# Splitting the second-layer matmuls of the two later parts into two 64-row matmuls with a PSUM bank each

## The chip, the cores and the metric

The kernel runs on one core of one Trainium2 chip. The metric is the device time of one execution in microseconds (us); lower is better.

## What is computed

The reference has two steps. The first is attention over q, k and v of shape (4, 8, 576, 64): four heads look at a local window of 32 positions, four at every 32nd position. The second is a mixture of four experts on the 2304 x 512 result, weighted by normalised domain probabilities. Almost all of the time is in the second step:

```python
p = domain_probs / (domain_probs.sum(-1, keepdims=True) + 1e-09)
for e in range(E):                     # E = 4, D = 512, F = 1024
    h = np.maximum(x @ w1[e], 0.0)     # (2304, 512) @ (512, 1024)
    out += p[:, e:e + 1] * (h @ w2[e]) # (2304, 1024) @ (1024, 512)
```

## The kernel before, in words

**Units and parts.** Each expert's hidden layer is cut into two halves of 512, so there are eight units of weights (a 512 x 512 piece of w1 and one of w2). The 2304 tokens are cut into three parts: a first of 512 tokens and two later ones of 896. The first part goes through all eight units while attention still runs. Then each later part goes through its eight units, so that there are sixteen stages of the kind below.

**Precision.** Every matmul operand is split into a high and a low part in the 4-byte type float32r, and a product is the sum of high x high, high x low and low x high. ScalarE writes the high parts (lines 616, 676, 787), VectorE or GpSimd the low ones (lines 617, 679, 788).

**A stage of a later part** (`plan_unit`, line 818) has two phases on TensorE. In the first phase the first layer is done by a seven-product scheme on quarter blocks (line 811): 7 products x 2 column blocks x 6 matmuls = 84 matmuls of 448 columns. ScalarE and VectorE then finish `h`: 16 tiles of 128 x 448 (four blocks of the hidden axis, two token halves, high and low). In the second phase each of the seven 128-token tiles `t` gets 12 matmuls of 512 columns (`mm2_t`, line 684): four blocks `f` of the hidden axis, three products each, all accumulated in one PSUM bank. The `h` slice is the stationary operand (128 rows x 128 columns), the `w2` block the moving one (128 rows x 512 columns). VectorE then reads the bank, scales it by the token's probability and adds it to `acc` (`accumulate`, line 690). After the last unit of a part SyncE sends `acc` out (line 720). The very last token tile of the kernel is done in two column halves of 256.

**Banks.** PSUM's eight banks are three pools: "mo" with four, "sc" with two and "ps" with two. `next_bank` (line 701) goes round them as mo, ps, mo, sc, and a bank is taken again when what read it is done.

**Order.** The order on every engine is written out ahead. `Plan` (line 32) simulates the engines with a duration and a due time for every operation. TensorE's matmuls of the two layers keep the order in which they are added. On the other engines the operation that can start first goes first, and the due time decides between several. Operations marked "VP" can go to VectorE or to GpSimd, whichever the simulation finishes earlier. The order that comes out is each engine's program.

**Attention** matters here as the only place before the change where matmuls use part of the array. Scores (line 460) are 64-row by 64-column matmuls that alternate between rows and output partitions 0 to 63 and 64 to 127. The value product of the strided heads (line 545) has 54 rows, which start at partition 0 for the first bank and at 64 for the second, and alternates between output partitions 0 to 63 and 64 to 127. The transposes of line 515 use all 128 rows. These operands are plain float32.

Of the kernel before, what the change touches and what calls it, by code (L numbers as in the profile page):

```python
# [31 lines left out]
class Plan:  # L32
# [19 lines left out]
    def add(self, eng, dur, fn, reads=(), writes=(), prio=0.0, bank=None, moe=False, cols=0, xfer=None, two=False, lead=None):  # L52

        o = Op()
        o.eng, o.dur, o.fn, o.prio, o.bank, o.moe = eng, dur, fn, prio, bank, moe  # L60
        o.start = None
        o.cols = cols
        o.xfer = xfer
        o.two = two or eng == "VP"
        o.ready = 0.0
        o.nxt = []
        o.idx = len(self.ops)
        pre = set()
        for r in reads:
            if r in self.writer:  # L70
                pre.add(self.writer[r])
        for w in writes:
            if w in self.writer:
                pre.add(self.writer[w])
            pre.update(self.readers.get(w, ()))
        pre.discard(o)
        for r in reads:
            self.readers.setdefault(r, []).append(o)
        for w in writes:
            self.writer[w] = o  # L80
            self.readers[w] = []
        o.kind, o.lead, o.early = eng, lead, 0.0
        o.wait = o.pre = len(pre)
        for p in pre:
            p.nxt.append(o)
        self.ops.append(o)
# [215 lines left out]
def attn_moe_kernel(  # L302
# [13 lines left out]
    nc = tc.nc  # L316
    B, H, S, D = 4, 8, 576, 64
    NT, DM = out.shape
    E, _, F = w1.shape
# [49 lines left out]
    def bank(key):  # L369
        t = pools[key[0]].tile([P, 512], F32, tag=key[0], name=key[0])  # L370
        held[key] = t
        return t
# [317 lines left out]
    def accumulate(a, g, e, key, first, cs):  # L690
        sc = pr[:, g, e:e + 1]
        a = a[:, cs]
        pt = held[key][:, 0:cs.stop - cs.start]
        if first:
            nc.vector.tensor_scalar_mul(out=a, in0=pt, scalar1=sc)
        else:
            nc.vector.scalar_tensor_tensor(out=a, in0=pt, scalar=sc, in1=a, op0=ALU.mult, op1=ALU.add)  # L697
# [3 lines left out]
    def next_bank():  # L701
        cnt[0] += 1
        return (("sc", "mo", "ps", "mo")[cnt[0] % 4], "s", cnt[0])

    def plan_mm2(key, hh, hl, htok, ts, a, g, e, first, last, z, cs=ALL):
        passes = list(enumerate((i, f) for f in range(NKF) for i in range(3)))
        for o in (0, 6):
            js = passes[o:o + 6]
            need = set()
            for _, (i, f) in js:  # L710
                need.update(htok("hhl"[i], f))
                need.add(f"w2{f}" + "hlh"[i])
            w = (cs.stop - cs.start) / DM
            add("PE", PT * w, lambda js=js: mm2_t(hh(), hl(), ts, js, key, cs), sorted(need), [key], z,
                key if o == 0 else None, True, 3072 * w)
        tok = f"acc{a}{cs.start}"
        toks = [tok] if cs != ALL or a < TB // P - 1 else [f"acc{a}{i}" for i in (0, DM // 2)]
        add("DVE", 0.75, lambda: accumulate(acc[a], g, units[e][0], key, first, cs), [key, "pr"], toks, z + 2 * PT)
        if last:
            add("SP", 0.4, lambda: nc.sync.dma_start(out=out[g * P:g * P + P, cs], in_=acc[a][:, cs]), toks,  # L720
                [f"out{g}{cs.start}"], z + 3, xfer=((0.8 * w, 128),))

    def plan_first(u, z):

        def mm1_op(f, js):
            key = ("mo", "a", u, f)
            need = set()
            for _, (i, c) in js:
                need.add((("a11", "a12"), ("s3", "a22"))[f // 2][c // 2] + "hhl"[i])
                need.update(f"x{'hlh'[i]}{c}{g}" for g in range(2))  # L730
            add("PE", (TA + 32) / 2400 * len(js), lambda: mm1_plain(f, js, key), sorted(need), [key], z,
                key if js[0][0] == 0 else None, True, TA * len(js))

        passes = list(enumerate(PASS if u else PASS0))
        if u == 0:
            for o in range(0, 12, 3):
                for f in range(NKF):
                    mm1_op(f, passes[o:o + 3])
        else:
            for f in range(NKF):  # L740
                mm1_op(f, passes)
        for f in range(NKF):
            key = ("mo", "a", u, f)
            src = lambda key=key: held[key][:, 0:TA]
            add("ACT", 0.62, lambda f=f, src=src: relu_hi(lambda: hs[0][f], src), [key], [f"hh{f}"], z)
            add("DVE", 0.68, lambda f=f, src=src: relu_lo(lambda: hs[1][f], lambda: hs[0][f], src),
                [key, f"hh{f}"], [f"hl{f}"], z)
        for t in range(TA // P):
            plan_mm2(("mo", "b", u, t), lambda: hs[0], lambda: hs[1], lambda j, f: [f"h{j}{f}"],
                     slice(t * P, t * P + P), t, t, u, u == 0, u == NU - 1, z + 11)  # L750
# [67 lines left out]
    def plan_unit(part, u, first, last, z):  # L818
        ka, kb, kc = ([next_bank() for _ in range(2)] for _ in range(3))
        SEQ = (("a11", "b11", ka, 1), ("s1", "t1", kc, 1), ("s2", "t2", ka, 0), ("a12", "b21", kb, 1),  # L820
               ("s3", "t3", ka, 0), ("a22", "t4", ka, 0), ("s4", "b22", kc, 0))
        us = {}

        def copy_u(nm, f, key, zz):
            i = us[nm, f] = ucnt[0] % 4
            ucnt[0] += 1
            add("ACT", 0.55, lambda: nc.scalar.activation(out=late["u"][i], in_=held[key][:, 0:TH], func=AF.Copy),  # L827
                [key, "late2"], [f"u{i}"], zz)

        def finish(f, half, key, nm, zz):  # L830

            cs = slice(half * TH, half * TH + TH)
            hi, lo = (lambda: late["h"][0][f][:, cs]), (lambda: late["h"][1][f][:, cs])
            need = [key]
            src = lambda: held[key][:, 0:TH]
            if nm:
                i = us[nm]
                c = ucnt[1] % 2
                ucnt[1] += 1
                add("DVE", 0.6, lambda: nc.vector.tensor_tensor(  # L840
                    out=late["c"][c], in0=held[key][:, 0:TH], in1=late["u"][i], op=ALU.add), [key, f"u{i}"], [f"c{c}"], zz)
                src = lambda: late["c"][c]
                need = [f"c{c}"]
            add("ACT", 0.52, lambda: relu_hi(hi, src), need + ["late2"], [f"Hh{f}{half}"], zz + 0.6)
            add("DVE", 0.6, lambda: relu_lo(lo, hi, src), need + [f"Hh{f}{half}"], [f"Hl{f}{half}"], zz + 1.1, two=bool(nm))

        for n, (a, b, keys, first_in) in enumerate(SEQ):
            for f in range(2):
                key = keys[f]
                zz = z + (2 * n + f) * PM  # L850
                need = [a + "h", a + "l"] + [f"{b}{h}{j}" for h in "hl" for j in range(2)]
                add("PE", PM, lambda a=a, b=b, f=f, key=key, first_in=first_in: product(a, b, f, key, first_in),
                    need, [key], zz, key if first_in else None, True, 6 * TH)
                ze = zz + PM
                if n == 0:
                    copy_u("p1", f, key, ze)
                elif n == 2:
                    copy_u("u2", f, key, ze)
                elif n == 3:
                    finish(f, 0, key, ("p1", f), ze)  # L860
                elif n == 4:
                    copy_u("u3", f, key, ze)
                    finish(2 + f, 1, kc[f], ("u3", f), ze)
                elif n == 5:
                    finish(2 + f, 0, key, None, ze)
                elif n == 6:
                    finish(f, 1, key, ("u2", f), ze)
        g0 = (TA + (part - 1) * TB) // P
        for t in range(TB // P):
            halves = sorted({t * P // TH, (t * P + P - 1) // TH})  # L870
            end = part == 2 and last and t == TB // P - 1
            for cs in (slice(0, DM // 2), slice(DM // 2, DM)) if end else (ALL,):
                plan_mm2(next_bank(), lambda: late["h"][0], lambda: late["h"][1], lambda j, f, halves=halves: [f"H{j}{f}{x}" for x in halves],
                         slice(t * P, t * P + P), t, g0 + t, u, first, last, z + 14 * PM + 2 * PT * t, cs)


# [142 lines left out]
```

## Time and profile before

| | before |
|---|---|
| median of 3 runs | 837.15 us (836.17 to 837.17) |
| the profiled execution, its own time | 836.88 us |
| its span, first to last instruction | 835.1 us |
| TensorE matmul busy | 826.3 us, 99% of the span, 4953 matmuls |
| VectorE busy | 507.1 us, 61%, 772 instructions |
| ScalarE, GpSimd busy | 325.5 us (39%), 219.4 us (26%) |
| TensorE clock granted | 0.999 of full speed |

How to read it: PE is TensorE's matmuls and PEld its weight loads, which overlap them; DVE is VectorE, ACT ScalarE, POOL GpSimd, SP SyncE. L688 means line 688 of the kernel. Successive matmuls overlap in the records, since each is drawn with its pipeline's tail, so the cadence is read from starts, or from a merged stretch by its count, and not from one matmul's duration. "128*128" behind a matmul is rows by columns of the stationary operand, the shape after it the moving one. A row of the timeline merges neighbours of one kind: start, length of the merged stretch, count at the end.

### The profile page before, as it was taken

What the parts mean: (1) busy time and instruction counts of PE and PEld (TensorE: products, weight loads), DVE (VectorE), ACT (ScalarE), POOL (GpSimd) and SP (SyncE); (2) the same over time, 40 slices, a digit from 0 to 9 for tenths busy, and PEclk for the clock granted to TensorE, in tenths of its full rate; (3) what the DMA queues carried; (4) which work ended last, traced back from release to release, by engine and by line L of the source; (5) the groups of instructions that cost most, each with busy time, mean ns of one, the idle gap of its engine ahead of it and who ended that gap; (6) DMA issues with size and microseconds to landing.
All of it is one profiled execution on the core that took longest, in us unless ns stands there. A gap on an engine that the chain in (4) does not pass through costs nothing.

```text
span 835.1 us, 12327 instructions
## 1 busy us (share of the span) xinstructions
PE 826.3 (99%) x4953; PEld 707.2 (85%) x4953; DVE 507.1 (61%) x772; ACT 325.5 (39%) x606; POOL 219.4 (26%) x187
## 2 busy tenths in 40 slices
PE   8999999999999999999999999999999999999998
PEld 5788887888889888888988889898888988888896
DVE  5987974845546474655747466664646656475552
ACT  4554455533325143351624326152442615234240
POOL 5632232701402130321313042521312213031100
PEclk9999999999999999999999999999999999999999
DMA  9754731323220121111212111111111113111002
GB/s 303 264 187 154 225 110 52 102 101 101 101 76 27 50 100 51 50 51 51 75 46 83 51 51 51 75 64 46 57 50 51 51 51 101 51 51 51 0 1 89
DMA packets 33114, 68.97 MB, mean 83 GB/s; under 512 B 2080, under 2 KB 2464, under 8 KB 33056
## 3 DMA queue, kind: packets, MB, share of 16 engines
q1 hardware_dynamic: 32624, 67.92, 24.1%
q8 instruction: 39, 0.64, 0.3%
q10 hardware_dynamic: 432, 0.26, 0.1%
q14 instruction: 19, 0.16, 0.1%
HBM read 63.45 MB, written 4.72 MB: 82 GB/s over the span
## 4 chain that ended last, share of the span: by engine, by line
PE 96%; DMA 3%; ACT 0%; issue 0%; DVE 0%
PE mo L688 29%; PE mo L811 16%; PE mo L672 10%; PE ps L688 9%; PE sc L688 9%; PE sc L811 8%; PE ps L811 8%; PE sc L460 2%; PE ps L545 2%; PE ps L515 2%; DMA raw<-in_w 1%; DMA vstL<-in_v_local 1%; DMA m_loc<-c_local 0%; ACT xr L592 0%; ACT w2h L616 0%
## 5 line engine op out<-in xcount | busy, mean ns | idle before, releaser
L688 PE MATMUL mo<-w2h,h 128*128 128x512 f32 (+1 forms) x456 | 148.7, 387 | 0.0
L616 ACT ACTIVATE w2h<-raw 128x512 fp32r<-128x512 f32 x88 | 54.9, 631 | 240.5 <-PE mo L688 136.0
L697 DVE SCALAR_TENSOR_TENSOR acc<-mo,pr,acc 128x512 f32<-128x512 f32 (+1 forms) x77 | 57.5, 746 | 89.8 <-PE mo L688 88.8
L688 PEld LDWEIGHTS mo<-w2h,h 128*128 128x128 f32 x456 | 85.4, 188 | 17.4
L679 DVE SCALAR_TENSOR_TENSOR h<-c,h 128x448 fp32r<-128x448 f32 x96 | 93.0, 993 | 6.8 <-ACT h L676 3.4
L688 PE MATMUL mo<-w2l,h 128*128 128x512 f32 (+1 forms) x228 | 88.3, 387 | 0.0
L617 POOL TENSOR_TENSOR w2l<-raw,w2h 128x512 fp32r<-128x512 f32 x25 | 34.0, 1365 | 196.7 <-ACT w2h L616 196.6
L688 PE MATMUL mo<-w2h,hs 128*128 128x512 f32 x256 | 83.0, 395 | 0.0
L617 POOL TENSOR_TENSOR a12l<-raw,a12h 128x512 fp32r<-128x512 f32 x18 | 29.7, 1648 | 167.4 <-ACT a12h L616 135.8
L688 PE MATMUL ps<-w2h,h 128*128 128x512 f32 x224 | 73.5, 389 | 0.0
L688 PE MATMUL sc<-w2h,h 128*128 128x512 f32 (+1 forms) x224 | 72.5, 385 | 0.0
L676 ACT ACTIVATE h<-c 128x448 fp32r<-128x448 f32 x96 | 52.8, 575 | 17.7 <-DVE c L840 15.7
L688 PEld LDWEIGHTS mo<-w2h,hs 128*128 128x128 f32 x256 | 48.0, 188 | 10.3
L617 DVE TENSOR_TENSOR w2l<-raw,w2h 128x512 fp32r<-128x512 f32 x63 | 44.7, 737 | 9.7 <-ACT w2h L616 9.7
L688 PEld LDWEIGHTS mo<-w2l,h 128*128 128x128 f32 x228 | 42.8, 188 | 8.5
L688 PE MATMUL mo<-w2l,hs 128*128 128x512 f32 x128 | 49.9, 390 | 0.0
L688 PEld LDWEIGHTS ps<-w2h,h 128*128 128x128 f32 x224 | 42.1, 188 | 8.7
L688 PEld LDWEIGHTS sc<-w2h,h 128*128 128x128 f32 x224 | 41.9, 188 | 8.4
L827 ACT ACTIVATE u<-mo 128x448 f32<-128x448 f32 x48 | 26.2, 545 | 50.7 <-PE mo L811 50.3
L688 PE MATMUL ps<-w2l,h 128*128 128x512 f32 x112 | 43.6, 389 | 0.0
L688 PE MATMUL sc<-w2l,h 128*128 128x512 f32 (+1 forms) x112 | 43.2, 385 | 0.0
L840 DVE TENSOR_TENSOR c<-mo,u 128x448 f32<-128x448 f32 x48 | 29.5, 615 | 17.7 <-PE mo L811 16.4
(278 smaller groups left out, 1713.0 us busy)
## 6 DMA issues: line engine op xcount, KB each, us to landing
raw<-in_w SPq DMA_DIRECT2D x44, 1024.0 KB, 5.3
qkS<-in_qk_strided SPq DMA_DIRECT2D x16, 329.0 KB, 8.0
out<-acc SPq DMA_DIRECT2D x17, 256.0 KB, 2.0
vstL<-in_v_local SPq DMA_DIRECT2D x8, 432.0 KB, 8.0
vstS<-in_v_strided SPq DMA_DIRECT2D x8, 384.0 KB, 9.0
qkL<-in_qk_local SPq DMA_DIRECT2D x8, 336.0 KB, 7.1
qkL<-in_qk_local SPq DMA_DIRECT2D x8, 272.0 KB, 7.3
out<-acc SPq DMA_DIRECT2D x2, 128.0 KB, 1.7
```

What stands on the lines that cost most here:

```text
L460: nc.tensor.matmul(s[a, o:o + W], lhsT, rhs, start=True, stop=True)
L515: nc.tensor.transpose(pt[0:rows, P * (g - g0):P * (g - g0) + P], src, ident)
L616: add("ACT", 0.62, lambda: nc.scalar.activation(out=hi(), in_=src(), func=AF.Copy), need, [name + "h"], z)
L617: add("VP", VP, lambda e: engine(e).tensor_tensor(out=lo(), in0=src(), in1=hi().bitcast(F32), op=ALU.subtract), need + [name + "h"], [name ...
L672: nc.tensor.matmul(pt[:, 0:TA], w[:, c % 2, (f % 2) * P:(f % 2) * P + P], (xl if i == 1 else xh)[c], start=j == 0, stop=j == 11)
L676: nc.scalar.activation(out=dst(), in_=src(), func=AF.Relu)
L679: nc.vector.scalar_tensor_tensor(out=dst(), in0=src(), scalar=0.0, in1=hi().bitcast(F32), op0=ALU.max, op1=ALU.subtract)
L688: nc.tensor.matmul(pt, ht[f][:, ts], wt[f][:, cs], start=j == 0, stop=j == 11)
L697: nc.vector.scalar_tensor_tensor(out=a, in0=pt, scalar=sc, in1=a, op0=ALU.mult, op1=ALU.add)
L811: nc.tensor.matmul(pt, wq[a][i == 2][:, j, f * P:f * P + P], xq[b][i == 1][j], start=bool(first) and n == 0, stop=True, skip_group_check=True)
L827: add("ACT", 0.55, lambda: nc.scalar.activation(out=late["u"][i], in_=held[key][:, 0:TH], func=AF.Copy), [key, "late2"], [f"u{i}"], zz)
L840: add("DVE", 0.6, lambda: nc.vector.tensor_tensor(out=late["c"][c], in0=held[key][:, 0:TH], in1=late["u"][i], op=ALU.add), [key, f"u{i}"], ...
```

## The change

A later part's token tile now takes two banks. Each of its 12 matmuls is written as two, over rows 0 to 63 and rows 64 to 127 of the same operands. The first accumulates in one bank, the second in the other, and they alternate. VectorE adds both banks to `acc`, one after the other. The first part keeps `plan_mm2`, and the planner is given the same TensorE duration for a pair as for the one matmul before.

```diff
+    def mm2_rows(hh, hl, ts, js, keys, cs):
+        pts = [(held[k] if k in held else bank(k))[:, 0:cs.stop - cs.start] for k in keys]
+        for j, (i, f) in js:
+            ht, wt = ((hh, w2h), (hh, w2l), (hl, w2h))[i]
+            for r, pt in enumerate(pts):
+                rows = slice(64 * r, 64 * r + 64)
+                nc.tensor.matmul(pt, ht[f][rows, ts], wt[f][rows, cs], start=j == 0, stop=j == 11)
+
+    def plan_mm2_rows(keys, hh, hl, htok, ts, a, g, e, first, last, z, cs=ALL):
...
+            if o == 0:
+                add("PE", 0.0, lambda: bank(keys[0]), (), [keys[0]], z, keys[0], True)
+            add("PE", PT * w, lambda js=js: mm2_rows(hh(), hl(), ts, js, keys, cs), sorted(need), list(keys), z,
+                keys[1] if o == 0 else None, True, 3072 * w)
...
+        for i, key in enumerate(keys):
+            add("DVE", 0.75, lambda i=i, key=key: accumulate(acc[a], g, units[e][0], key, first and i == 0, cs), [key, "pr"], toks, z + 2 * PT)
...
-                plan_mm2(next_bank(), lambda: late["h"][0], lambda: late["h"][1], lambda j, f, halves=halves: [f"H{j}{f}{x}" for x in halves],
+                plan_mm2_rows((next_bank(), next_bank()), lambda: late["h"][0], lambda: late["h"][1], lambda j, f, halves=halves: [f"H{j}{f}{x}" for x in halves],
                          slice(t * P, t * P + P), t, g0 + t, u, first, last, z + 14 * PM + 2 * PT * t, cs)
```

## Rows read from the trace of the kernel before

**Rows 1.** The page: span, busy time, and the granted clock in 40 slices.

```profile
span 835.1 us, 12327 instructions
PE 826.3 (99%) x4953; PEld 707.2 (85%) x4953; DVE 507.1 (61%) x772; ACT 325.5 (39%) x606; POOL 219.4 (26%) x187
PEclk9999999999999999999999999999999999999999
```

**Rows 2.** Busy time by phase: a second layer, a first layer, the last first layer.

```profile
core 0: us, PE busy (x) PEld busy (x) DVE busy (x) ACT busy (x) POOL busy (x), PEclk, DMA share, GB/s
269.59:288.64 19.05, 19.05 (x85) 15.77 (x84) 9.55 (x13) 3.26 (x6) 3.18 (x4) 1.00 0.17 56
288.64:305.76 17.12, 17.12 (x86) 15.77 (x85) 12.07 (x18) 10.57 (x21) 4.96 (x4) 1.00 0.19 63
...
794.98:812.09 17.11, 17.11 (x86) 15.76 (x84) 8.46 (x14) 7.58 (x15) 0.89 (x1) 1.00 0.00 1
```

**Rows 3.** Line 688 alone, from the first stage to the last matmul.

```profile
252.48:831.50 579.02, 307.79 (x1357) 253.08 (x1356) 1.00 0.16 54
```

**Rows 4.** The chain that ended last, its final pieces: start us, us, what.

```profile
825.86 2.72 PE mo L688 x12
828.58 1.43 PE sc L688 x12
830.02 1.45 PE mo L688 x12
831.47 0.02 issue
831.49 0.48 DVE acc L697
```

**Rows 5.** The timeline inside a second layer: matmuls and the weight loads beside them.

```profile
599.87 0.19 PEld L688 LDWEIGHTS mo<-w2l,h 128*128 128x128 f32 x1
600.09 0.39 PE L688 MATMUL mo<-w2l,h 128*128 128x512 f32 x1
600.09 0.19 PEld L688 LDWEIGHTS mo<-w2h,h 128*128 128x128 f32 x1
...
600.32 0.39 PE L688 MATMUL mo<-w2h,h 128*128 128x512 f32 x1
```

**Rows 6.** The timeline in attention: partial-array matmuls, and full-row transposes.

```profile
56.67 0.27 PE L515 MATMUL ps<-ident,pmS 128*128 128x128 f32 x1
56.87 1.61 PE L460 MATMUL sc<-qkS 64*64 64x54 f32 x48
...
58.79 0.60 PE L515 MATMUL ps<-ident,pmL 128*96 128x128 f32 x4
...
75.80 0.22 PE L545 MATMUL ps<-pTS,vstS 54*64 54x54 f32 x1
...
35.83 0.80 PE L545 MATMUL ps<-pTS,vstS 54*64 54x54 f32 x28
```

**Rows 7.** The timeline where TensorE goes from line 688 to 545 and back.

```profile
137.54 0.39 PE L688 MATMUL mo<-w2l,hs 128*128 128x512 f32 x1
...
137.76 0.40 PE L688 MATMUL mo<-w2h,hs 128*128 128x512 f32 x1
138.09 0.38 PE L545 MATMUL ps<-pTS,vstS 54*64 54x54 f32 x6
...
139.12 0.40 PE L545 MATMUL ps<-pTS,vstS 54*64 54x54 f32 x8
...
139.45 0.50 PE L688 MATMUL mo<-w2h,hs 128*128 128x512 f32 x1
...
139.78 0.39 PE L688 MATMUL mo<-w2l,hs 128*128 128x512 f32 x1
```

**Rows 8.** Line 697 in the later parts: durations in ns (min/median/max), first and last start.

```profile
L697 DVE SCALAR_TENSOR_TENSOR acc<-mo,pr,acc x51: 483/751/752, 250.0 to 831.5; 128x512 f32<-128x512 f32 x50, 128x256 f32<-128x256 f32 x1
```

More of the change, by code (lines that the diff above doesn't have):

```diff
@@ L721, in plan_mm2 @@
                 [f"out{g}{cs.start}"], z + 3, xfer=((0.8 * w, 128),))
+    def mm2_rows(hh, hl, ts, js, keys, cs):
[6 more added lines that the diff above has]
+    def plan_mm2_rows(keys, hh, hl, htok, ts, a, g, e, first, last, z, cs=ALL):
+        passes = list(enumerate((i, f) for f in range(NKF) for i in range(3)))
+        w = (cs.stop - cs.start) / DM
+        for o in (0, 6):
+            js = passes[o:o + 6]
+            need = set()
+            for _, (i, f) in js:
+                need.update(htok("hhl"[i], f))
+                need.add(f"w2{f}" + "hlh"[i])
+            if o == 0:
+                add("PE", 0.0, lambda: bank(keys[0]), (), [keys[0]], z, keys[0], True)
+            add("PE", PT * w, lambda js=js: mm2_rows(hh(), hl(), ts, js, keys, cs), sorted(need), list(keys), z,
+                keys[1] if o == 0 else None, True, 3072 * w)
+        tok = f"acc{a}{cs.start}"
+        toks = [tok] if cs != ALL or a < TB // P - 1 else [f"acc{a}{i}" for i in (0, DM // 2)]
+        for i, key in enumerate(keys):
+            add("DVE", 0.75, lambda i=i, key=key: accumulate(acc[a], g, units[e][0], key, first and i == 0, cs), [key, "pr"], toks, z + 2 * PT)
+        if last:
+            add("SP", 0.4, lambda: nc.sync.dma_start(out=out[g * P:g * P + P, cs], in_=acc[a][:, cs]), toks,
+                [f"out{g}{cs.start}"], z + 3, xfer=((0.8 * w, 128),))
     def plan_first(u, z):
```

## The prediction, made before the change was run

> **What bounds the kernel now.** I read the page first. TensorE's matmuls are busy 826.3 of 835.1 us at the full clock, and no other engine passes 61% [rows 1]. So the time is the sum of TensorE's cadences, and the question is what a matmul costs in the stretch that changes. The busy times by phase show the pattern there: a second layer lasts 19.05 us and a first layer 17.1 us, TensorE is busy throughout both, and VectorE works 9.55 us of the second layer and 12.07 us of the first [rows 2]. There are sixteen such stages. Line 688 alone accounts for 307.79 us in them, with 1356 matmuls (one more hangs over the window's edge) [rows 3]. Of these 1332 have 512 columns and 24, those of the last token tile, have 256.
>
> The chain that ended last gives the cadence without the overlap in which matmuls are drawn. Twelve matmuls of 512 columns take 2.72 us, 0.2267 us each, and twelve of 256 columns 1.43 to 1.45 us, 0.120 us each [rows 4]. The difference, 0.1067 us for 256 columns, is 0.417 ns per column, so 512 columns take 213.3 ns, and **13.3 ns of each matmul do not depend on its columns**. That is the only part of the cadence that a new way of writing the matmul could save: 1356 x 13.3 ns = 18.0 us. The weight load is not exposed beyond that. Each load of 0.19 us starts together with the matmul before its own (both at 600.09) and ends inside the 0.227 us [rows 5].
>
> **The change, part by part.**
>
> *The pairs.* Each of the 1356 matmuls becomes two with the same columns and half the rows. No row shows this form in float32r. The nearest ones are attention's. There a full-row transpose of 128 columns follows the one before after (0.60 - 0.27) / 3 = 0.11 us, or 0.86 ns per column; by that a 54-column matmul alone would take 46 ns. The 64-row, 64-column matmuls follow each other after (1.61 - 0.22) / 47 = 29.6 ns, so two are in the array at once. In the stretch at 35.83 they follow after (0.80 - 0.22) / 27 = 21.5 ns [rows 6]. One row half holds only two column tiles, so a cadence under half of 46 ns there needs rows from 0 and rows from 64 at work together, into the same output partitions of two banks. That is just what the change writes. I therefore take a pair to last as long as the one matmul did: the two halves stream side by side, each with its 13.3 ns. The term is 0. Its lower bound is -18.0 us, the whole fixed part gone. Its upper bound is one after the other: 1332 x 0.2267 + 24 x 0.120 = +304.8 us. I stay at 0 because it is what the nearest rows show, and the two ends are cases of their own below.
>
> The Trainium skill ("TensorE: Matmul & The Clock Gate", Part 3, "Measured speedup vs the span model") adds about 4 ns for each further tile of a set. By that the sum would be 1356 x 4 ns = 5.4 us higher, an estimate of 848.8 us. No run here shows it for float32r, and the sum goes without it.
>
> *Changing form.* Where TensorE goes from full-row to partial matmuls and back it loses time. The first 54-row matmul starts 0.33 us after the last full one (137.76 to 138.09) instead of 0.227, a loss of 0.10. On the way back the last partial one starts at 139.12 + 0.40 - 0.22 = 139.30 and the full one at 139.45, 0.15 us instead of a pair's 0.06, a loss of 0.09; and the second full one comes 0.33 us after the first instead of 0.227, a loss of 0.10, its load having had nothing to hide behind [rows 7]. I take that last loss for the first pair too. Going in costs 0.20 us and coming out 0.19. Both phases run in order within a stage, so there are 16 ways in and 15 out: 16 x 0.20 + 15 x 0.19 = **+6.05 us**, all on TensorE's path. The bounds are 0 (halves of the rows at full width need no such pause) and twice that, 12.1 us.
>
> *VectorE.* Each token tile gets a second accumulation of 0.75 us [rows 8]: 7 x 0.75 = 5.3 us per second layer, which brings VectorE from 9.55 to 14.8 of 19.05 us. Its idle time hides this, and I cost it at 0. Both accumulations wait for the same last matmul, so the second adds no wait, only 0.75 us to whatever stands behind it: low parts of the next weights, which can go to GpSimd (3.18 us busy there), and the last additions for `h`, needed by the fourth tile, three tiles of 2.72 us after the phase begins. A tile's two banks are asked for again four tiles later, 10.9 us, while the accumulations take 1.5 us. In the last first layer, where VectorE has little help, it works 8.46 of 17.11 us [rows 2]. If one accumulation per stage were uncovered after all, that would be 16 x 0.75 = 12 us; nothing in this part can gain.
>
> *SyncE and the end.* An output waits for both accumulations. Between the parts that puts the weight load behind it in SyncE's queue at most 0.75 us later, which has most of a first layer to spare. At the very end nothing covers it: after the last matmul VectorE does one accumulation of 256 columns, 0.48 us [rows 4], and now two: **+0.48 us**.
>
> *Sum.* 836.88 (the profiled execution; the median of the runs is 837.15, 0.03% above) + 0 + 6.05 + 0 + 0.48 = **843.4 us**. About 0.2% (1.7 us) is what a measurement of this kernel can tell from no change, and this is 0.8%.
>
> **The rivals.**
>
> *Float32r halves do not run together.* A float32r stream takes a column every 0.417 ns, twice the rate of attention's float32 ones at 0.86 ns [rows 4, 6]. Four of the slow streams at once ask for no more columns than two of the fast ones, which speaks against this rival, but no row has two fast ones. The split would then buy nothing, and the time is 836.9 + 304.8 + 0.5 = 1142 us. Chance 0.16.
>
> *The fixed part is paid twice in a pair.* If the 13.3 ns belong to something that both halves share, the second half's comes on top: 836.9 + 18.0 + 6.05 + 0.5 = 861.4 us. Attention's pairs show no second pause, but there each float32 matmul moves at half the rate. Chance 0.12.
>
> *The fixed part disappears*, the one that ends on the other side. If the 13.3 ns are the array waiting to change weights that are already loaded, one half can stream while the other changes: 836.9 - 18.0 + 6.05 + 0.5 = 825.4 us. It decides as soon as it saves more than 4.8 of the 13.3 ns (6.5 us / 1356). Against it: each half alone still has its own pause, and two that start together pause together. Chance 0.20. The Trainium skill has a rule for this side (the same page, Part 3, "The mechanism"): a weight load overlaps a running matmul only when their row groups differ. Taken literally, loads were exposed before and hidden after. The trace disagrees, since the load of 0.19 us already lies under a full-row matmul [rows 5]; what is left for the rule is at most this rival's 18.0 us.
>
> **How the numbers follow.** The forecast holds 0.50 and has a range of its own of 837 to 855 us: no pauses at one end, doubled pauses or an uncovered accumulation per stage at the other. The three rivals hold 0.48, and 0.02 is left for a VectorE that falls further behind. The time is that of the forecast, 843.4 us. The range from 824 to 866 us takes in the forecast, the vanished and the doubled fixed part, together 0.82, and leaves out the halves in sequence. Faster is the vanished fixed part, less the little of it that would only pay for the pauses: 0.19. Within 0.2% needs no pauses, or a small part of the 13.3 ns saved: 0.05. Slower is the rest, 0.76.
>
> **What would show it.** In the profile after, the cadence of a pair says most. Twelve pairs in 2.72 us confirm the term of 0; 2.56 us is the vanished fixed part, 2.88 us the doubled one, 5.4 us the sequence. The first layer should stay at 17.1 us plus the pause on the way back, and VectorE should rise by about 84 us in all (111 x 0.75 + 2 x 0.48). The two halves should start a few ns apart. The prediction is wrong if a second layer lasts under 19.0 or over 19.7 us, if TensorE is seen waiting for VectorE in it, or if the form changes cost nothing.

## The result and the profile after

| | before | after |
|---|---|---|
| median of the runs | 837.15 us | 843.30 us (843.00 to 844.62) |
| ratio, 95% interval | | 1.0081 [1.0058, 1.0104] |
| the profiled execution, its own time | 836.88 us | 844.62 us |
| its span | 835.1 us | 842.8 us |
| first stage begins / last matmul ends | 252.48 / 831.45 us | 253.56 / 838.64 us |

The change made the kernel slower by 0.8%, 6.2 us between the medians; the forecast was 843.4 us.

The page after, its span and busy times (as in [rows 1]):

```profile
span 842.8 us, 15284 instructions
PE 832.5 (99%) x6306; PEld 704.5 (84%) x6309; DVE 577.0 (68%) x857; ACT 325.6 (39%) x606; POOL 254.5 (30%) x215
```

Busy time by phase after: a second layer, a first layer, the last first layer, with the columns of [rows 2].

```profile
270.75:290.02 19.27, 19.27 (x170) 15.67 (x169) 13.02 (x18) 3.28 (x6) 4.82 (x5) 1.00 0.17 56
290.02:307.31 17.29, 17.29 (x86) 15.68 (x84) 12.66 (x18) 10.52 (x21) 6.27 (x5) 1.00 0.17 61
801.86:819.15 17.29, 17.29 (x86) 15.68 (x84) 9.04 (x14) 7.56 (x15) 2.10 (x2) 1.00 0.00 1
```

There are twice as many matmuls in a second layer, but by the starts it lasts only 0.21 us longer (19.262 against 19.055), and a first layer 0.19 us longer (17.298 against 17.112). By its busy time TensorE never idles in either, since each matmul is drawn with its tail; what is lost shows in the starts alone. VectorE has gone from 9.55 to 13.02 us of the second layer (the forecast was 14.8), and from 8.46 to 9.04 us of the last first layer, where it has the least help; it keeps TensorE waiting in neither. The timeline, TensorE alone, shows where the 0.21 and 0.19 us come from. The first view is the way into a second layer, the second the way out of it. The view rounds to 10 ns and merges neighbours; the intervals named below are between starts in the trace, to the ns.

```profile
599.30 0.56 PE L840 MATMUL ps<-b22h,s4l 128*128 128x448 f32 x2
599.79 0.50 PE L729 MATMUL mo<-w2h,h 64*128 64x512 f32 x1
599.80 0.50 PE L729 MATMUL sc<-w2h,h 64*128 64x512 f32 x1
600.13 0.39 PE L729 MATMUL mo<-w2l,h 64*128 64x512 f32 x1
600.13 0.39 PE L729 MATMUL sc<-w2l,h 64*128 64x512 f32 x1
600.37 0.39 PE L729 MATMUL mo<-w2h,h 64*128 64x512 f32 x1
600.37 0.39 PE L729 MATMUL sc<-w2h,h 64*128 64x512 f32 x1
```

```profile
618.51 0.39 PE L729 MATMUL mo<-w2l,h 64*128 64x512 f32 x1
618.51 0.39 PE L729 MATMUL sc<-w2l,h 64*128 64x512 f32 x1
618.74 0.39 PE L729 MATMUL mo<-w2h,h 64*128 64x512 f32 x1
618.74 0.39 PE L729 MATMUL sc<-w2h,h 64*128 64x512 f32 x1
619.06 0.68 PE L840 MATMUL mo<-b11h,a11h 128*128 128x448 f32 x2
619.57 0.57 PE L840 MATMUL mo<-b11l,a11h 128*128 128x448 f32 x2
```

The two halves of a pair, "mo" and "sc" here, start 3 to 4 ns apart in the records, and pairs follow every 0.23 us, as single matmuls did before. At the two borders TensorE pauses. On the way in the first pair starts 0.290 us after the last first-layer matmul (0.206 before the change), and the second pair 0.337 us after the first (0.235 before). On the way out the full-row matmul starts 0.315 us after the pair before it (0.227 before), and its successor 0.307 us later (0.206 before). So each border has a pause, 0.084 and 0.088 us, and a late second matmul, 0.10 us each.

The weight loads beside them show more of the late second matmul. The same border before and after, with lines left out:

```profile
269.18 0.57 PE L811 MATMUL ps<-b22h,s4l 128*128 128x448 f32 x2
269.38 0.19 PEld L688 LDWEIGHTS mo<-w2h,h 128*128 128x128 f32 x1
...
269.59 0.40 PE L688 MATMUL mo<-w2h,h 128*128 128x512 f32 x1
269.59 0.19 PEld L688 LDWEIGHTS mo<-w2l,h 128*128 128x128 f32 x1
```

```profile
270.26 0.56 PE L840 MATMUL ps<-b22h,s4l 128*128 128x448 f32 x2
...
270.75 0.18 PEld L729 LDWEIGHTS mo<-w2h,h 64*128 64x128 f32 x1 [0.30 <-issue]
270.75 0.50 PE L729 MATMUL mo<-w2h,h 64*128 64x512 f32 x1
...
270.86 0.19 PEld L729 LDWEIGHTS mo<-w2l,h 64*128 64x128 f32 x1
...
271.09 0.39 PE L729 MATMUL mo<-w2l,h 64*128 64x512 f32 x1
```

Before, the load of the second layer's first matmul starts with the last first-layer matmul (269.38), and the next load with that first matmul. After, no load is recorded beside the last first-layer matmul (270.46). The first pair's loads, before which the loads stood idle for 0.30 us with nothing in the profile to wait for, are recorded with the pair itself, and the second pair's start 0.107 us after it, 0.104 later than in the stream. The second pair is as late, 0.102 us. On the way out it is the same (0.106 us).

The end of the timeline, VectorE's last two accumulations (before there was one, [rows 4]):

```profile
838.67 0.48 DVE L697 SCALAR_TENSOR_TENSOR acc<-mo,pr,acc 128x256 f32<-128x256 f32 x1 [0.28 <-PE ps L729]
839.26 0.48 DVE L697 SCALAR_TENSOR_TENSOR acc<-ps,pr,acc 128x256 f32<-128x256 f32 x1
```

From the start of the first stage to the end of the last matmul it is 585.08 us against 578.98, 6.10 us more: the sixteen first layers together 2.87 us, the sixteen second layers 3.23 us. From the last matmul to the end it is 4.20 us against 3.62, 0.58 more. The rest of the 7.7 us by which the profiled executions differ, 1.08 us, arose before the first stage. There TensorE's program differs only in three fewer matmuls on the filler tile `wz`, 18 instead of 21, all before 19 us. The waits of TensorE after have this row, where before the same wait lasted 0.3 us:

```profile
PE ps L545 <- issue: 1.3, 1, 1.3
```

Over the twelve profiles of this study, the kernel before among them, the first stage begins between 251.75 and 256.35 us. So single executions are compared below from there on, by the phases. Part of that movement goes with TensorE's granted clock, as the first run below shows.

### The profile page after: what moved, and what is told of

It reads as the page before. It is cut to its first block, busy times and chain, and to the rows that moved or that the text cites. A ratio compares the mean times of both kernels' runs of the same rounds, so it can differ in the third digit from the quotient of the medians.

```text
span 842.8 us, 15284 instructions
## 1 busy us (share of the span) xinstructions
PE 832.5 (99%) x6306; PEld 704.5 (84%) x6309; DVE 577.0 (68%) x857; ACT 325.6 (39%) x606; POOL 254.5 (30%) x215
## 4 chain that ended last, share of the span: by engine, by line
PE 96%; DMA 3%; ACT 0%; issue 0%; DVE 0%; DVEq 0%
PE mo L729 36%; PE mo L840 17%; PE ps L840 14%; PE mo L688 11%; PE mo L672 10%; PE sc L460 2%; PE sc L840 2%; PE ps L545 2%; DMA raw<-in_w 2%; PE ps L515 2%; DMA vstL<-in_v_local 1%; DMA m_loc<-c_local 0%; PE sc L729 0%; PE ps L729 0%; DVE acc L697 0%
## 5 line engine op out<-in xcount | busy, mean ns | idle before, releaser
L729 PE MATMUL mo<-w2h,h 64*128 64x512 f32 (+1 forms) x904 | 279.3, 386 | 0.0
L729 PEld LDWEIGHTS mo<-w2h,h 64*128 64x128 f32 x904 | 165.9, 184 | 39.5 <-issue 4.8
L729 PE MATMUL mo<-w2l,h 64*128 64x512 f32 (+1 forms) x452 | 173.8, 385 | 0.0
L729 PE MATMUL sc<-w2h,h 64*128 64x512 f32 (+1 forms) x512 | 167.9, 388 | 0.0
L729 PE MATMUL ps<-w2h,h 64*128 64x512 f32 (+1 forms) x392 | 126.9, 384 | 0.0
L729 PE MATMUL sc<-w2l,h 64*128 64x512 f32 (+1 forms) x256 | 98.6, 385 | 0.0
L729 PEld LDWEIGHTS mo<-w2l,h 64*128 64x128 f32 x452 | 83.2, 184 | 16.9
L729 PEld LDWEIGHTS sc<-w2h,h 64*128 64x128 f32 x512 | 94.0, 184 | 0.0
L729 PE MATMUL ps<-w2l,h 64*128 64x512 f32 (+1 forms) x196 | 75.2, 384 | 0.0
L729 PEld LDWEIGHTS ps<-w2h,h 64*128 64x128 f32 x392 | 72.0, 184 | 0.0
L688 PEld LDWEIGHTS mo<-w2h,hs 128*128 128x128 f32 x256 | 48.1, 188 | 10.2
```

Source lines behind the costliest of these rows:

```text
L688: nc.tensor.matmul(pt, ht[f][:, ts], wt[f][:, cs], start=j == 0, stop=j == 11)
L729: nc.tensor.matmul(pt, ht[f][rows, ts], wt[f][rows, cs], start=j == 0, stop=j == 11)
```

## The experiments

Ratios are to runs of the kernel before on the same chip. A profile's sums over all sixteen first layers and all sixteen second layers are from the first matmul of a phase to the first of the next, for the last phase to its last matmul's start. One half alone in the second layer, the blocks of six and of twelve and the quarters were executed once each and have no ratio.

**The change again.** The kernel as it is.

> The change as it is, once more. Theory: 843.0 us give or take 0.5, ratio 1.007 to 1.008; second layers of 19.26 us, first layers of 17.30 us, and 4.2 us from the last matmul to the end. The 1.3 us in which TensorE waited for no engine at 76.8 us in the first profile belong to that execution and should not come back at the same place.

Measured: 844.46 us median (843.09 to 847.07), ratio 1.0078 [1.0056, 1.0101]. The first layers take 276.66 us, the second layers 308.14 us and the end 4.20 us, equal to the first profile of the change to 0.01 us. The wait of 1.3 us did not come back. The stage began at 255.76 us this time, 2.2 us later, and here TensorE's granted clock was at the lower of its two levels (1.2 GHz, 0.50 of full speed) from 17.78 to 28.02 us, where in the first profile it was at 2.4 GHz:

```profile
17.78:28.02 10.24, 9.72 (x109) 8.06 (x110) 7.88 (x19) 5.64 (x13) 8.14 (x9) 0.50 1.00 361
```

TensorE had waited 1.25 us at 14.1 and 0.40 at 16.7 us before it fell; in the first profile the waits of 1.44 us at 14.3 and 0.33 at 17.1 were followed by no fall, so what decides is not shown. The three of the six executions with a mean clock of 1.000 took 843.1 to 843.5 us, the two with 0.993 took 846.85 and 847.07.

**VectorE and the banks alone.** Full rows, six matmuls into each bank, both banks accumulated.

```diff
-            for r, pt in enumerate(pts):
-                rows = slice(64 * r, 64 * r + 64)
-                nc.tensor.matmul(pt, ht[f][rows, ts], wt[f][rows, cs], start=j == 0, stop=j == 11)
+            nc.tensor.matmul(pts[j // 6], ht[f][:, ts], wt[f][:, cs], start=j % 6 == 0, stop=j % 6 == 5)
```

> The change without its row halves: full-row matmuls as before, but the first six of a token tile go to one bank and the last six to the other, and both banks are accumulated as in the change. Theory (the loss is the change of form between full rows and row halves, and VectorE's second accumulation is hidden): no change of form, so a second layer stays at 19.05 us, a first layer at 17.1 us, and the time is that of the kernel before plus one 256-column accumulation at the end, 0.5 us: 837.4 to 838.0 us, ratio 1.0006. Rival (VectorE's 84 us more, or the doubled use of banks, cost the 6 us): 843 us, ratio 1.007, with TensorE waiting for VectorE in the second layers.

Measured: 838.77 us (836.44 to 843.22), ratio 1.0018 [1.0000, 1.0035]. Its busy time by phase, a second and a first layer:

```profile
269.17:288.23 19.06, 19.06 (x86) 15.77 (x85) 13.54 (x19) 3.27 (x6) 4.80 (x5) 1.00 0.17 56
288.23:305.34 17.11, 17.11 (x86) 15.77 (x85) 12.74 (x18) 10.53 (x21) 6.26 (x5) 1.00 0.19 63
```

VectorE works 13.54 us of the second layer, more than in the change, and the phase lasts what it did before. The sums are 273.79 and 304.91 us, those of the kernel before. So the second accumulation and the doubled banks cost nothing in the stages. The 0.5 us at the end did not come either (3.62 us), because here the first bank is full six matmuls earlier and its accumulation is done in time. The interval of the ratio reaches down to 1; what it shows above that is not in the stages of this profile, the shortest of the twelve executions. The rest goes with the granted clock: the five executions with a mean of 0.991 to 0.996 took 840.3 to 843.2 us, the seven with 0.998 to 1.000 took 836.4 to 839.0.

**One accumulation.** The other half of the same question.

```diff
-        for i, key in enumerate(keys):
+        for i, key in enumerate(keys[:1]):
```

> The change without its second accumulation: the second bank is filled and never read, so the output lacks the upper row half's share in the two later parts. Theory: the changes of form stay, 6.1 us, and only the 0.5 us at the end go: 843 us, ratio 1.0073, second layers of 19.26 us. Rival (VectorE costs it): back to 837.2 to 838 us, ratio 1.000 to 1.001.

Measured: 843.41 us, ratio 1.0069 [1.0052, 1.0085]; 276.66 and 308.14 us, exactly the change's; the end takes 3.65 us. The loss in the stages stays without the second accumulation, and the 0.55 us at the end go, as forecast.

**One tile of seven in row halves.**

```diff
+                split = t == 3
-                plan_mm2_rows((next_bank(), next_bank()), ...
+                (plan_mm2_rows if split else plan_mm2)((next_bank(), next_bank()) if split else next_bank(), ...
```

> Row halves for the fourth token tile of each stage alone, the other six as before. Theory (each change of form costs about 0.19 us, whatever lies between): 16 stages with one way in and one way out, 16 x (0.20 + 0.19) = 6.2 us, as much as the whole change although only a seventh of the pairs is there, and nothing at the end: 843 us, ratio 1.0075. Rival (each pair or each second accumulation costs a little, 6.1 us / 112 tiles): 16 tiles, 0.9 us: 838 us, ratio 1.001.

Measured: 845.39 us, ratio 1.0096 [1.0078, 1.0114]. A seventh of the pairs costs more than all of them did. The first layers are as before (273.79 us). A second layer, for which the columns are those above, lasts 0.49 us more than 19.05:

```profile
270.72:290.27 19.55, 19.55 (x97) 15.61 (x96) 10.13 (x14) 3.27 (x6) 3.17 (x4) 1.00 0.17 54
```

Sixteen times that is 7.9 us, the second layers' 312.80 less 304.91. The price goes with the borders, two in a stage, and not with the pairs. It was larger than forecast, 0.25 us a border. The timeline shows the same pause and the same late second matmul, and then this for the way out:

```profile
318.30 0.39 PE L729 MATMUL sc<-w2h,h 64*128 64x512 f32 x1
318.30 0.39 PE L729 MATMUL mo<-w2h,h 64*128 64x512 f32 x1
318.62 0.50 PE L688 MATMUL ps<-w2h,h 128*128 128x512 f32 x1
318.95 0.40 PE L688 MATMUL ps<-w2l,h 128*128 128x512 f32 x1
319.19 0.63 PE L688 MATMUL ps<-w2h,h 128*128 128x512 f32 x2
```

The full-row matmuls that follow come after 0.335, 0.235, 0.233 and 0.236 us: besides the pause, the next few stay some ns above 0.227. At the start of a second layer that settling was there before the change too (0.235 and 0.233 us after the first two matmuls), so the change pays it only in part.

**Every other tile.** Eight borders in a stage.

```diff
+                split = t % 2 == 0
```

> Row halves for token tiles 0, 2, 4 and 6 of each stage, full rows for 1, 3 and 5: eight changes of form in a stage instead of two, with fewer pairs. Theory: 64 ways in at 0.20 us and 63 out at 0.19 us, 24.8 us, and 0.5 us at the end: 862 us, ratio 1.030. Rival (a cost per pair or per second accumulation): four sevenths of 6.1 us, 841 us, ratio 1.004.

Measured: 866.85 us, ratio 1.0346 [1.0324, 1.0368]. Second layers last 20.74 us, 1.48 us more than the change's for six more borders, 0.25 us each, as with one tile. The direction and the growth with the number of borders are as the theory has them; the sum was 5 us short, because 0.195 us a border is about the price at the edge of a first layer, not that between two runs of 512 columns.

**One half alone in the second layer.**

```diff
...
-                plan_mm2_rows((next_bank(), next_bank()), ...
+                plan_mm2_rows((next_bank(),), ...
```

> The row halves 0 to 63 alone: every second-layer matmul of the two later parts has only its lower half, one bank, one accumulation, so the upper half of each contraction is left out. Theory (a half alone has the full cadence of 0.2267 us, and in the change the second half rides along free): no time saved, 843 us, twelve matmuls in 2.72 us. Rival A (a half costs half, and the pair ran in sequence): twelve in 1.36 us, 1356 x 0.113 us less, 690 us. Rival B (the two halves share the 13.3 ns that do not depend on the columns, and one alone would not have them): twelve in 2.56 us, 825 us.

Measured: 843.34 us. The chain of the first three tiles of a second layer, start us, us, what:

```profile
270.43 2.94 PE mo L729 x12
273.37 2.72 PE sc L729 x12
276.08 2.72 PE mo L729 x12
```

Twelve half matmuls take what twelve full ones did. In the change the upper half rides along free, and leaving it out gives nothing back; the 13.3 ns beyond the columns belong to each half by itself. The 2.94 us of the first tile hold the pause and the late second matmul of the way in. From the start of the first stage to the end of the last matmul it is 584.77 us, against 585.08 in the change: the price of the borders stays with one half, one bank and one accumulation.

**One half alone in both layers.** The same, and the first layer's matmuls cut to rows 0 to 63 too.

```diff
-                    pt, wq[a][i == 2][:, j, f * P:f * P + P], xq[b][i == 1][j], ...
+                    pt, wq[a][i == 2][0:64, j, f * P:f * P + P], xq[b][i == 1][j][0:64, :], ...
```

> Row halves 0 to 63 alone in both layers of the two later parts, so the upper half of every contraction there is left out, and TensorE keeps one form from the first stage to the end. Theory (what the change costs is the change of form between the phases): one change of form in all instead of 31, second layers back at 19.05 us and first layers at 17.11 us or a little less, 837 us, ratio 1.000, against 843.3 us with the lower half in the second layer alone. Rival (matmuls of 64 rows start or end a phase more slowly whatever stands beside them): 843 us, ratio 1.007.

Measured: 837.44 us, ratio 0.9991 [0.9974, 1.0007]. A second and a first layer:

```profile
269.51:288.57 19.06, 19.06 (x86) 15.46 (x84) 9.34 (x13) 3.27 (x6) 3.17 (x4) 1.00 0.18 56
288.57:305.68 17.11, 17.11 (x86) 15.47 (x84) 12.07 (x18) 10.54 (x21) 4.95 (x4) 1.00 0.17 63
```

With one form throughout, both phases are back at 19.06 and 17.11 us although every matmul in them has 64 rows. Against the run before this one, which differs by the rows of the first layer alone, that stretch is 5.7 us shorter (579.08 against 584.77). It is 0.10 us longer than in the kernel before, all of it in the very first first layer, behind the one change of form that is left. It shows that the cost is the change of form and not the form.

**Blocks of six.** The pairs of the change, not alternating: six lower halves, then six upper ones, twice a tile.

```diff
-        for j, (i, f) in js:
-            ...
-            for r, pt in enumerate(pts):
-                rows = slice(64 * r, 64 * r + 64)
+        for r, pt in enumerate(pts):
+            rows = slice(64 * r, 64 * r + 64)
+            for j, (i, f) in js:
+                ht, wt = ((hh, w2h), (hh, w2l), (hl, w2h))[i]
```

> The same matmuls as in the change in another order: six lower halves, then six upper halves, twice a token tile, instead of alternating. Theory (matmuls start in program order, a row half takes one at a time, and only neighbours in different halves run together): each of the four blocks of a tile has six starts in sequence, and the last of a block overlaps the first of the next: 24 matmuls cost about 20 cadences instead of 12, 112 x 8 x 0.2267 = 203 us more than the change: about 1047 us (1150 us if nothing overlaps at the block ends). Rival (the engine looks far enough ahead to run the two blocks side by side): 843 us as the change.

Measured: 853.58 us. The theory's 1047 us were far off. The timeline at the start of a second layer, lower halves in "mo", upper ones in "sc":

```profile
268.96 0.50 PE L729 MATMUL mo<-w2h,h 64*128 64x512 f32 x1
269.30 0.39 PE L729 MATMUL mo<-w2l,h 64*128 64x512 f32 x1
269.54 0.39 PE L729 MATMUL mo<-w2h,h 64*128 64x512 f32 x1
269.54 0.49 PE L729 MATMUL sc<-w2h,h 64*128 64x512 f32 x1
269.77 0.39 PE L729 MATMUL mo<-w2h,h 64*128 64x512 f32 x1
269.88 0.39 PE L729 MATMUL sc<-w2l,h 64*128 64x512 f32 x1
270.00 0.39 PE L729 MATMUL mo<-w2l,h 64*128 64x512 f32 x1
```

The first upper half is the seventh matmul in program order. It starts 6 ns after the third, before the fourth to sixth. From there the halves run side by side, 0.11 us out of step at first, each at a cadence of its own, 0.227 us in the lower and about 0.231 in the upper. A second layer lasts 19.96 us, 0.70 more than in the change: the upper half starts 0.58 us late, and at the end its last three matmuls run alone (3 x 0.227 us). So matmuls of different row groups start out of program order here. The Trainium skill ("TensorE: Matmul & The Clock Gate", Part 3, "The mechanism") has matmuls start and end strictly in program order; this trace disagrees for different row groups.

**Blocks of twelve.** The same with a whole tile's twelve. Besides the order of the blocks of six:

```diff
-        for o in (0, 6):
-            js = passes[o:o + 6]
+        for o in (0,):
+            js = passes
...
```

> All twelve lower halves of a token tile, then all twelve upper ones. The blocks of six ran side by side, the upper one starting when the third lower matmul started, so the engine looks ahead of what is running. Theory (it looks about four matmuls ahead, since the seventh in program order started just after the third): the thirteenth starts just after the ninth, four of a block overlap with the next block, 16 cadences a tile instead of 12: 112 x 4 x 0.2267 = 102 us more than the change, about 945 us. Rival A (it looks ahead a dozen or more): the blocks run side by side but for a start, 845 to 860 us. Rival B (only the ends of blocks overlap, and the blocks of six did so for another reason): 22 cadences a tile, 1097 us.

Measured: 987.99 us. The timeline of the first tile:

```profile
270.66 0.39 PE L729 MATMUL mo<-w2l,h 64*128 64x512 f32 x1
270.89 0.39 PE L729 MATMUL mo<-w2h,h 64*128 64x512 f32 x1
270.89 0.49 PE L729 MATMUL sc<-w2h,h 64*128 64x512 f32 x1
271.11 0.39 PE L729 MATMUL mo<-w2h,h 64*128 64x512 f32 x1
```

The first "sc" is the thirteenth matmul and starts with the ninth, as expected from four ahead. The same holds all along: in the fifteen stages with 512 columns throughout, each of the 195 blocks that follow another starts 6 to 8 ns after the ninth matmul of the one before. The time lies between the theory's 945 and rival B's 1097 us, though four of twelve do overlap as expected. The theory mis-sized two other things. From block to block it is 1.955 us and not eight cadences, 1.813, because in each block the second matmul comes 0.335 us after the first and some of the others a few ns late: with 14 blocks a stage, about 32 us in all. And the last block of a stage has no next one to overlap with, 16 x 4 x 0.2267 = 14.5 us. The theory's 102 us with these two is 148; the second layers take 146 us more than in the change.

**Quarters.** Four matmuls of 32 rows, four banks, four accumulations.

```diff
-                rows = slice(64 * r, 64 * r + 64)
+                rows = slice(32 * r, 32 * r + 32)
...
-                plan_mm2_rows((next_bank(), next_bank()), ...
+                plan_mm2_rows(tuple(next_bank() for _ in range(4)), ...
```

> Four matmuls of 32 rows into four banks, all four accumulated. Theory (row groups run side by side as long as their banks are free, and VectorE's cover then ends): a set of four still has the cadence of 0.2267 us, but a tile's four accumulations take 3.0 us against 2.72 us of matmuls, VectorE is asked for 9.55 + 3 x 5.25 = 25.3 us in a second layer of 19 us, and TensorE waits for banks: 860 to 940 us, with VectorE near 90% busy in the later parts. Rival (only two row groups run together): twelve sets in at least 5.4 us, 1150 us or more.

Measured: 902.42 us. A second layer, and the longest waits of TensorE's loads in the stages (who waited for whom: us in total, times, longest):

```profile
311.92:334.16 22.24, 21.18 (x337) 17.20 (x336) 19.94 (x28) 3.23 (x6) 6.39 (x6) 1.00 0.14 49
```

```profile
PEld ps L729 <- DVE acc L697: 25.5, 41, 0.7
PEld sc L729 <- DVE acc L697: 24.7, 40, 0.7
```

Sets of four follow each other every 0.227 us as pairs and single matmuls do. But from the third tile of a stage on TensorE waits for a bank that VectorE has not yet emptied; VectorE is busy 90% of the phase. So VectorE's cover, which held in the change, ends between two and four accumulations a tile.

## Why the prediction was right

*The pairs at no cost.* Held, and sharply. A pair, a half and a set of four quarters all have the full-row matmul's cadence, 0.227 us. The starts of two halves are 3 to 4 ns apart, but the next pair does not come later for it, so the sum by the rows held. The 4 ns for a further tile of the Trainium skill ("TensorE: Matmul & The Clock Gate", Part 3, "Measured speedup vs the span model") show in the starts and not in the cadence of a stream; its sum, 848.8 us, was the worse one.

*The changes of form, 6.05 us.* Measured 6.10 us: 0.084 and 0.10 us on the way in, 0.088 and 0.10 us on the way out, where the prediction had 0.10, 0.10, 0.09 and 0.10. By these four the sum would be 5.8 us. The other 0.3 us, which the prediction did not have, are in the next few pairs of a second layer, which come some ns later than the matmuls there did before. That the two deviations cancel to 0.05 us is luck; the mechanism and the size of each term were right. That these are paid per border is shown from three sides: more borders cost more (two against eight in a stage), fewer pairs with the same borders do not cost less, and the same half-row matmuls without borders cost nothing. That the second matmul is late by its load is borne out in part: its load starts 0.10 us late, as the rows above show. Why it does, and that the pause is the array emptying, is not shown; the rows show only where the time lies.

*VectorE hidden.* Held. It cost nothing in the stages, shown by adding it without the row halves and by taking it out of them. The accumulations did take 84.3 us more, as forecast, but VectorE as a whole rose by 69.9 us only, because the planner moved work to GpSimd: 14 low parts of `w2` (GpSimd wrote 25 before and 39 after; VectorE's time for them fell by 4.3 us), as the prediction allowed for, and 12 of the sums of weight blocks for the first layer's scheme (`tmp<-tmp,raw`, 10.2 us), which it did not name. GpSimd rose by 35.1 us, from 219.4 [rows 1] to 254.5.

*The end, 0.48 us.* Measured 0.58 us; with one accumulation it is 0.04. The second accumulation itself takes the forecast 0.48 us; it starts 0.10 us after the first one's end.

*The rivals.* Halves in sequence and a doubled fixed part fall by the cadence of the pair. The vanished fixed part falls too, and by more than its argument in the prediction: even halves that run 0.11 us and more out of step, so that one could stream while the other changes weights, each keep 0.227 us or more. Blocks of six showed this by accident.

*What the sum did not contain.* The agreement of 843.4 with 843.3 us is closer than the method: the part before the first stage moves by up to 4.6 us between executions. By the phases the predicted 6.5 us stand against 6.7 measured.

## What to carry to other kernels

Splitting a matmul's rows buys nothing where the full array was already in use: the halves run side by side, each at the cadence of the whole, and the second bank has to be added by another engine. Where the row halves stand between full-row matmuls, count the borders, at 0.20 to 0.25 us each here, and not the matmuls. A second accumulation is free only while the engine that does it has room in that phase: at 13 of 19 us VectorE still had, with four accumulations a tile it had not.

## What was not expected of the hardware

Matmuls of different row halves start ahead of earlier ones in the program: the seventh with the third, the thirteenth with the ninth, four ahead in both. So halves need not be alternated one by one to run side by side; blocks of six cost 0.70 us a stage for their late start, blocks of twelve 9.1 us a stage (28.39 against 19.26).

Float32r runs in groups of 64 and of 32 rows with the full width of 128 columns, at the same cadence as full rows, up to four at a time into four banks. And a border between two runs of 512 columns costs 0.25 us, while one at the edge of the first layer costs 0.20 (6.10 us / 31): the next few matmuls also come some ns late, which at that edge they did in part before.
